# A long convolution on one Trainium2 core: its first step folded over the sign of j and run as four 64 by 64 tiles

## The chip, the cores and the metric

The kernel runs on one core of a Trainium2 chip. The core has five engines that work side by side and wait for each other through semaphores: TensorE (PE in the profile; PEld is its loading of weights), VectorE (DVE), ScalarE (ACT), GpSimd (POOL) and SyncE (SP), which here only issues DMAs. The metric is the device time of one execution in microseconds. A profile is one execution with the hardware profiler on; its span runs from the first to the last instruction.

## The reference

A gated long convolution is followed by a soft mixture of experts over its output. Only the convolution is touched by the change.

```python
h_mlp = np.maximum(pos_emb @ w1, 0.0) @ w2          # S x D filter, S = 11456, D = 128
h_filt = h_mlp * np.exp(-0.01 * np.arange(S))[:, None]
u = x * v                                           # B x S x D, B = 4
y = irfft(rfft(u, n=2*S, axis=1) * rfft(h_filt, n=2*S, axis=0)[None], n=2*S, axis=1)[:, :S]
attn_out = x * y
# then a soft mixture of 8 experts over the B*S rows of attn_out
```

All numbers are fp32.

## The kernel before

**The transform.** A cyclic length of 111 times 197 replaces the FFT. A sequence position is written as 111 j + r + base with j from -52 to 52 (JT = 105 values) and r from 0 to 55 (R = 56), together with its mirror in r. So the input is already folded over the sign of r: `xf` and `vf` hold for each channel a column of 56 values at +r and one at -r. Four steps follow for each group g of 16 channels (CG = 16, with 4 batches C = 64 columns; 8 groups):

- Step 1 (`p1_load`, `p1`): x times v, then sum and difference of the +r and -r columns (`sd`), then a matmul over j against a table of cosines and sines with 99 frequencies k (J = 99). One unit u is 4 columns; a group has 16 units.
- Step 2 (`p2`): for each k one matmul over r with the table W, then the product with the filter's spectrum: two products on VectorE (`m`), a difference and a sum on GpSimd that go back into T. KB = 4 frequencies are one block, so a group has 25 blocks.
- Step 3 (`p3`): the inverse of step 2's sum; 32 calls in a group, two columns each. It takes sums and differences on the way to the big buffer E.
- Step 4 (`p4`): the inverse over k; 14 calls in a group, two for each of 7 blocks rb of 8 values of r. The result is multiplied by x (`xi`) and stored (`p4_out`) to the scratch tensor `scr`.

**The order.** The program runs a loop over g from 0 to 8. In a pass with g from 1 to 7 there are two halves. In the first, unit after unit, step 3 of group g-1 (two calls) stands beside step 1 of group g. In the second, step 4 of group g-1 stands beside step 2 of group g. T is shared: step 1 writes it, step 2 reads it and writes its own result there, step 3 reads that. So step 2 waits for all of step 1, and step 3 of the next pass needs every block of step 2. Before the passes stand the filter's own transform (`hid_step`, `first` with the table `tab1h`, `filter_second`) and group 0, which has only steps 1 and 2 (with `filter_last`, which makes the spectrum). The pass with g = 8 has only steps 3 and 4 of group 7. Behind it runs the mixture of experts.

Within this order a scheduler places the instructions of each engine by its estimate; where the code says `inorder`, program order is kept.

**Buffers.** `ld` holds 5 tiles that x, v and xi share; `st` holds 3 that sd and the outputs xo share. PSUM has two pools of 4 banks: `psa` for steps 1 and 2, `psb` for steps 3 and 4. SyncE issues nearly every DMA from one queue in order, so a load whose buffer isn't free yet holds up what stands behind it.

**How step 1 leaves PSUM.** `first` runs two matmuls with a 105 x 128 weight (56 sums and 56 differences, each padded to 64) against 198 columns (99 cosines, 99 sines). ScalarE then copies in three pieces: lines 130 and 131, and line 135 with the sign turned. For the filter and group 0 the third piece goes to VectorE (line 133).

**How an fp32 matmul looks in the trace.** Each fp32 matmul leaves two records on PE and two on PEld, called passes here: step 3 has 1024 matmuls in the program and 2048 passes.

## Time and profile before

| | us |
|---|---|
| median of 3 runs | 1148.19 (1145.26 to 1152.42) |
| the profiled execution | 1159.05 |
| its span | 1156.9 |
| filter, first step (24.8 to 70.9 of the span) | 46.1 |
| filter, second step (70.9 to 94.7) | 23.8 |
| first half of pass 1 (steps 3 and 1) | 52.4 |
| second half of pass 1 (steps 4 and 2) | 47.4 |
| from the start of pass 1 to the start of pass 8 (7 passes) | 710.0 |
| the mixture of experts (951.9 to the end) | 205.0 |

The borders are the first matmuls of the steps. The profiled execution took 1159.05 us, of which 1156.9 lie between the first and the last instruction; it is 0.9% above the median of the runs. The mixture of experts isn't touched by the change.

The lines that carry the argument stand in the prediction. A group's line gives the line of the kernel, engine, operation, what it writes and reads, shapes, count, then busy time in total and the mean of one, then the engine's idle time before it and who ended it. A line of windows gives for a stretch its length, then each engine's busy time with the number of instructions, the granted TensorE clock, the share of the DMA engines and their rate.

### The profile page before, as it was taken

How to read it: one execution, taken by the hardware profiler on the slowest of the kernel's cores; microseconds unless marked ns; L12 is line 12 of the kernel's file. 1: busy time of each engine (PE TensorE's matmuls, PEld its weight loads, DVE VectorE, ACT ScalarE, POOL GpSimd, SP SyncE). 2: the span in 40 equal slices, each digit the busy share in tenths (PEclk: the TensorE clock that was granted, in tenths of full speed). 3: DMA queues.
4: the chain of work that ended last, by engine and by line, in shares of the span. 5: the costliest groups of instructions: out<-in, count | busy, mean ns of one | idle time of the engine just before them, and what ended most of it. 6: DMA issues, size and time to landing. Idle time of an engine off the chain costs nothing.

```text
span 1156.9 us, 25846 instructions
## 1 busy us (share of the span) xinstructions
PE 1076.8 (93%) x9133; PEld 1005.2 (87%) x9133; DVE 895.9 (77%) x1835; ACT 603.8 (52%) x1496; POOL 603.1 (52%) x742
## 2 busy tenths in 40 slices
PE   6998998999999999999999999999999988997997
PEld 6888898999999899988989998998999986565675
DVE  6336886978779787877977786797778848997797
ACT  1978875920860392087039208703920308776597
POOL 6102486357437544743754474375447004776774
PEclk9689998999999999999999999999999999999998
DMA  8422368624734572474458247345824779774388
GB/s 289 121 80 88 124 228 249 202 79 136 209 112 125 159 229 72 135 210 119 123 154 235 84 133 212 117 125 160 221 80 148 242 208 277 221 220 124 124 353 338
DMA packets 129498, 198.49 MB, mean 172 GB/s; under 512 B 15926, under 2 KB 71537, under 8 KB 129372
## 3 DMA queue, kind: packets, MB, share of 16 engines
q1 hardware_dynamic: 129070, 196.61, 55.7%
q8 instruction: 74, 1.21, 0.5%
q14 instruction: 52, 0.43, 0.1%
q10 hardware_dynamic: 254, 0.11, 0.0%
q0 software_dynamic: 48, 0.13, 0.0%
HBM read 136.90 MB, written 59.90 MB: 170 GB/s over the span
## 4 chain that ended last, share of the span: by engine, by line
PE 40%; issue 21%; DVE 16%; DMA 10%; ACT 9%; POOL 4%; SPq 1%; POOLq 0%; DVEq 0%; ACTq 0%
PE p L284 8%; PE p L236 8%; DMA v<-in_vf_dram 8%; PE p L254 7%; PE p L126 6%; DVE E L260 5%; ACT T L130 4%; PE fl L168 3%; POOL x L218 3%; ACT T L131 3%; PE f L141 2%; PE ct L722 2%; DVE sd L221 2%; DVE xreg L433 2%; DVE xreg L738 1%
## 5 line engine op out<-in xcount | busy, mean ns | idle before, releaser
L258 ACT ACTIVATE ec<-p 99x224 f32<-99x224 f32 x256 | 84.0, 356 | 405.3 <-issue 341.5
L260 DVE TENSOR_TENSOR E<-p,ec 99x224 f32<-99x224 f32 x512 | 221.9, 550 | 43.3 <-ACT ec L258 42.7
L247 POOL TENSOR_TENSOR T<-m,m 111x256 f32<-111x256 f32 (+1 forms) x200 | 146.2, 731 | 187.5 <-DVE m L241 135.8
L241 DVE TENSOR_TENSOR m<-p,T 111x512 f32<-111x512 f32 (+1 forms) x350 | 216.0, 678 | 24.5 <-issue 16.3
L254 PE MATMUL p<-tab,T 111*99 111x112 f32 x2048 | 222.0, 262 | 8.7 <-DVE E L260 4.5
L254 PEld LDWEIGHTS p<-tab,T 111*99 111x99 f32 x2048 | 214.5, 171 | 14.5 <-issue 7.1
L218 POOL TENSOR_TENSOR x<-x,v 112x512 f32<-112x512 f32 x112 | 144.6, 1291 | 157.6 <-DMA v<-in_vf_dram 139.6
L284 PE MATMUL p<-E,tab 99*105 99x128 f32 (+1 forms) x1792 | 215.7, 276 | 11.5 <-DVE E L260 11.5
L126 PE MATMUL p<-tab1x,sd 105*128 105x198 f32 x1024 | 200.8, 342 | 18.7 <-DVE sd L221 16.4
L284 PEld LDWEIGHTS p<-E,tab 99*105 99x105 f32 x1792 | 205.4, 173 | 13.8 <-DVE E L260 11.4
L236 PE MATMUL p<-T,W 128*111 128x128 f32 x1584 | 202.2, 280 | 1.4 <-DVE T L133 1.4
L126 PEld LDWEIGHTS p<-tab1x,sd 105*128 105x128 f32 x1024 | 172.0, 194 | 25.7 <-DVE sd L221 13.0
L236 PEld LDWEIGHTS p<-T,W 128*111 128x111 f32 x1584 | 192.2, 178 | 1.6 <-DVE T L133 1.6
L130 ACT ACTIVATE T<-p 64x396 f32<-64x396 f32 x288 | 163.5, 568 | 33.6 <-PE p L126 29.0
L248 POOL TENSOR_TENSOR T<-m,m 111x256 f32<-111x256 f32 (+1 forms) x200 | 156.7, 783 | 0.0
L221 DVE TENSOR_TENSOR sd<-x 112x256 f32<-112x256 f32 x256 | 113.8, 484 | 55.2 <-POOL x L218 46.1
L290 DVE TENSOR_TENSOR xo<-p,xi 105x256 f32<-105x256 f32 x224 | 84.2, 417 | 47.7 <-PE p L284 34.9
L131 ACT ACTIVATE T<-p 64x198 f32<-64x198 f32 x288 | 106.1, 368 | 3.4
L135 ACT ACTIVATE T<-p 64x198 f32<-64x198 f32 x224 | 74.2, 331 | 0.0
L540 POOL TENSOR_TENSOR E<-lt,mx 128x480 f32<-128x480 f32 (+1 forms) x24 | 24.6, 1026 | 70.0 <-ACT et L522 67.0
L133 DVE TENSOR_SCALAR T<-p 64x198 f32<-64x198 f32 x64 | 27.1, 431 | 43.0 <-ACT T L131 42.5
L726 ACT ACTIVATE cs<-ct 96x512 fp32r<-96x512 f32 x96 | 53.3, 567 | 9.9 <-PE ct L722 6.6
(103 smaller groups left out, 1249.3 us busy)
## 6 DMA issues: line engine op xcount, KB each, us to landing
x<-in_xf_dram SPq DMA_DIRECT2D x128, 224.0 KB
v<-in_vf_dram SPq DMA_DIRECT2D x112, 224.0 KB
xi<-in_xi_dram SPq DMA_DIRECT2D x112, 224.0 KB
out_dram<-xreg SPq DMA_DIRECT2D x22, 960.0 KB
xreg<-scr SPq DMA_DIRECT2D x21, 960.0 KB
scr<-xo SPq DMA_DIRECT2D x104, 192.0 KB
hs<-E SPq DMA_DIRECT2D x12, 1024.0 KB
T<-hs SPq DMA_DIRECT2D x63, 176.0 KB
```

The source lines that it names most:

```text
L126: nc.tensor.matmul(ps[:, i].rearrange("p s k -> p (s k)"), lhsT=src(i), rhs=tab, start=True, stop=True)
L130: nc.scalar.activation(to[0:RP], pq[0:RP], AF.Copy)
L131: nc.scalar.activation(to[RP:128, 0], pq[RP:128, 1], AF.Copy)
L218: inorder(eng.tensor_tensor(out=xt, in0=xt, in1=vt, op=ALU.mult))
L221: add = nc.vector.tensor_tensor(out=sd[:, :, h : h + RP], in0=xt[:, :, 0:RP], in1=xt[:, :, RP:], op=op)
L236: nc.tensor.matmul(ps[:, i].rearrange("p b c -> p (b c)"), lhsT=W[:, k0 + i, :], rhs=Tf[:, :, k0 + i, :], start=True, stop=True)
L241: nc.vector.tensor_mul(m[:, :n].rearrange("p k s c i -> p k (s c i)").rearrange("p k (b c) -> p k b c", c=CG), ps[:, :n], h[:, :, CG * s : ...
L247: nc.gpsimd.tensor_tensor(out=Ty[:, 0], in0=ms[0][:, :n, 0], in1=ms[1][:, :n, 1], op=ALU.subtract)
L248: nc.gpsimd.tensor_tensor(out=Ty[:, 1], in0=ms[1][:, :n, 0], in1=ms[0][:, :n, 1], op=ALU.add)
L254: nc.tensor.matmul(ps[:, i, 2 * s : 2 * s + 2, :].rearrange("p q r -> p (q r)"), lhsT=T[0:N1, s, c // CG, c % CG // 2, :, i], rhs=tab3[:, ...
L260: add = nc.vector.tensor_tensor(out=E[:J, :, 2 * s : 2 * s + 2, c : c + 2].rearrange("p r q c -> p c q r"), in0=ps[:, :, 0:2, :], in1=ec, ...
L284: nc.tensor.matmul(ps[:, i, :n], lhsT=tab4[:, s, o : o + JT], rhs=E[:J, r, s : s + 2 * n - 1 : 2, :], start=(s == 0), stop=(s == 1))
```

## The change

Step 1 is folded over the sign of j too. x times v is followed by two rounds of sum and difference: over the sign of r (from xt into vt) and over the sign of j (from vt back into xt). What is left of j are 53 values (JH), so a unit is a tile of two rows of partitions: columns 0 and 1 in partitions 0 to 52, columns 2 and 3 in partitions 64 to 116. Each column's parts (even or odd in j, even or odd in r) need only the cosines or only the sines: 16 matmuls of 64 x 64 weights against 99 columns in a unit, each at a `tile_position` (64 i, 64 d), instead of 4 of 128 weights against 198. The two rows of tiles write two PSUM banks; the signs lie in the table, which has a third block of negative cosines. ScalarE copies a whole column pair at once.

The filter's `first` splits its 128 weights into two column tiles of 64, whose second reads a shifted table, so that no sign is turned behind it (`filter_first`, four functions f in a call).

Step 3 keeps its even and odd parts: PSUM goes to E with one copy, every third call on VectorE, the others on ScalarE. The sum and difference move behind step 4: ScalarE copies the odd part, VectorE adds and subtracts, and the product with x is one instruction for 8 values of r, on VectorE for the first output and on GpSimd for the second.

Buffers: `ld` has 4, `st` has 4 and takes v, psa has 2 tiles of two banks, and two blocks of step 2 share one.

```diff
-    ld = ctx.enter_context(tc.tile_pool(name="ld", bufs=5))
-    st = ctx.enter_context(tc.tile_pool(name="st", bufs=3))
+    ld = ctx.enter_context(tc.tile_pool(name="ld", bufs=4))
+    st = ctx.enter_context(tc.tile_pool(name="st", bufs=4))
...
-    psa = ctx.enter_context(tc.tile_pool(name="psa", bufs=4, space=bass.MemoryType.PSUM))
+    psa = ctx.enter_context(tc.tile_pool(name="psa", bufs=2, space=bass.MemoryType.PSUM))
...
+    def first(src, tab, ps):
+
+        for h in range(2):
+            nc.tensor.matmul(ps[64 * h : 64 * h + 64], lhsT=src[:, (R - 8) * h : (R - 8) * h + 64],
+                             rhs=tab[:, J * h : J * h + 2 * J], start=True, stop=True,
+                             tile_position=(0, 64 * h))
+
+    def filter_first(f0):
+        ps = psa.tile([128, 2, 512], F32, tag="psa", name=f"f1_{f0}")
+        for h in range(2):
+            for i in range(2):
+                f = f0 + 2 * h + i
+                first(hid[:, :, :, f].rearrange("p s r -> p (s r)"), tab1h,
+                      ps[:, h, 2 * J * i : 2 * J * (i + 1)])
+            f = f0 + 2 * h
+            nc.scalar.activation(Th.rearrange("p k (s f) -> p s k f", s=2)[:, :, :, f : f + 2],
+                                 ps[:, h, : 4 * J].rearrange("p (i s k) -> p s k i", i=2, s=2), AF.Copy)
...
+        shape = [128, 2, 2, 2, R]
+        xt = ld.tile(shape, F32, tag="ld", name=f"x_{g}_{u}")
...
+        vt = st.tile(shape, F32, tag="st", name=f"v_{g}_{u}")
...
-        for h, op in ((0, ALU.add), (RP, ALU.subtract)):
-            add = nc.vector.tensor_tensor(out=sd[:, :, h : h + RP], in0=xt[:, :, 0:RP], in1=xt[:, :, RP:],
-                                          op=op)
...
+        for a, b in ((xt, vt), (vt.rearrange("p c j s r -> p c s j r"), xt.rearrange("p c j s r -> p c s j r"))):
+            for h, op in ((0, ALU.add), (1, ALU.subtract)):
+                add = nc.vector.tensor_tensor(out=b[:, :, :, h], in0=a[:, :, :, 0], in1=a[:, :, :, 1], op=op)
...
     def p1(g, u, sd):
-        for h in range(0, 4, 2):
-            first(lambda i: sd[:JT, h + i, :], tab1x, T[:, :, u // 4, 2 * (u % 4) + h // 2], g == 0)
+        ps = psa.tile([128, 2, 512], F32, tag="psa", name=f"p1_{g}_{u}")
+        for c in range(2):
+
+            for e, d in ((0, 0), (1, 0), (1, 1), (0, 1)):
+                for i in range(2):
+                    w = sd[64 * i : 64 * i + JH, c, e].rearrange("p s r -> p (s r)")
+                    k = 2 * J * c + J * (e ^ d)
+                    nc.tensor.matmul(ps[64 * d : 64 * d + 64, i, k : k + J],
+                                     lhsT=w[:, (R - 8) * d : (R - 8) * d + 64],
+                                     rhs=tab1x[64 * i : 64 * i + JH, J * (e + 2 * (d > e)) : J * (e + 2 * (d > e)) + J],
+                                     start=True, stop=True, tile_position=(64 * i, 64 * d))
+        b, cp0 = u // 4, 2 * (u % 4)
+        for c in range(2):
+            nc.scalar.activation(T[:, :, b, cp0 + c],
+                                 ps[:, :, 2 * J * c : 2 * J * (c + 1)].rearrange("p i (s k) -> p s k i", s=2),
+                                 AF.Copy)
...
-        ec = sm.tile([J, 2, 2, R], F32, tag="ec", name=f"ec_{g}_{c}")
-        nc.scalar.activation(ec, ps[:, :, 2:4, :], AF.Copy)
...
+        to = E[:J, :, :, c : c + 2].rearrange("p r q c -> p q r c")
+        src = ps.rearrange("p c q r -> p q r c")
+        if c // 2 % 3 == 2:
+            nc.vector.tensor_copy(out=to, in_=src)
+        else:
+            nc.scalar.activation(to, src, AF.Copy)
...
+        vt = sm.tile([JT, 4, C], F32, tag="ec", name=f"odd_{g}_{rb}_{h}")
+        nc.scalar.activation(vt, ps[:, :, 1, :], AF.Copy)
+        for s, op in ((0, ALU.add), (1, ALU.subtract)):
+            nc.vector.tensor_tensor(
+                out=xo[s][:, :, 4 * h : 4 * h + 4, :].rearrange("p b r c -> p r b c"),
+                in0=ps[:, :, 0, :].rearrange("p r (b c) -> p r b c", b=B),
+                in1=vt.rearrange("p r (b c) -> p r b c", b=B), op=op)
+        if h:
+            for s, eng in ((0, nc.vector), (1, nc.gpsimd)):
+                eng.tensor_tensor(out=xo[s], in0=xo[s], in1=xs[s][:JT], op=ALU.mult)
```

In the lists below, a name such as `p_0_16_1871` is a tile of PSUM with its group, its column and a running number; `x4` counts matmuls in a row.

TensorE in the first half of pass 1, before: two calls of step 3 (line 254, 8 matmuls), then one unit of step 1 (line 126, 4 matmuls of the full array).

```order
L254 MATMUL p_0_16_1871<-tab_79,T 99x112 x4
L254 MATMUL p_0_18_1880<-tab_79,T 99x112 x4
L126 MATMUL p_72_1889<-tab1x,sd_4_1791 128x198 x2
L126 MATMUL p_73_1895<-tab1x,sd_4_1791 128x198 x2
L254 MATMUL p_0_20_1910<-tab_79,T 99x112 x4
```

The same place now:

```order
L271 MATMUL p_0_16_2000<-tab_82,T 99x112 x4
L271 MATMUL p_0_18_2006<-tab_82,T 99x112 x4
L234 MATMUL p_1_4_2012<-tab1x,x_4_1910 64x99 x16
L271 MATMUL p_0_20_2041<-tab_82,T 99x112 x4
L271 MATMUL p_0_22_2047<-tab_82,T 99x112 x4
```

Each unit's matmuls now stand as 16 small ones in one piece between the full-array matmuls of step 3, so the array changes between full and tiled twice in a unit.

GpSimd at the end of the second half of a pass, before: the last blocks of step 2 (lines 247 and 248, into T), then the products x times v of the next group (line 218).

```order
L247 TENSOR_TENSOR T<-m_2_88_3869,m_2_88_3871 111x4x32x2
L248 TENSOR_TENSOR T<-m_2_88_3871,m_2_88_3869 111x4x32x2
L247 TENSOR_TENSOR T<-m_2_92_3880,m_2_92_3882 111x4x32x2
L248 TENSOR_TENSOR T<-m_2_92_3882,m_2_92_3880 111x4x32x2
L247 TENSOR_TENSOR T<-m_2_96_3890,m_2_96_3892 111x3x32x2
L248 TENSOR_TENSOR T<-m_2_96_3892,m_2_96_3890 111x3x32x2
L218 TENSOR_TENSOR x_0_3930<-x_0_3930,v_0_3932 112x512
L218 TENSOR_TENSOR x_1_3938<-x_1_3938,v_1_3940 112x512
```

The same place now:

```order
L264 TENSOR_TENSOR T<-m_2_88_4106,m_2_88_4108 111x4x32x2
L265 TENSOR_TENSOR T<-m_2_88_4108,m_2_88_4106 111x4x32x2
L309 TENSOR_TENSOR xo_2_6_4138<-xo_2_6_4138,xi_1_6_4084 105x512
L218 TENSOR_TENSOR x_0_4172<-x_0_4172,v_0_4174 128x448
L218 TENSOR_TENSOR x_1_4181<-x_1_4181,v_1_4183 128x448
L264 TENSOR_TENSOR T<-m_2_92_4116,m_2_92_4118 111x4x32x2
L265 TENSOR_TENSOR T<-m_2_92_4118,m_2_92_4116 111x4x32x2
L264 TENSOR_TENSOR T<-m_2_96_4126,m_2_96_4128 111x3x32x2
L265 TENSOR_TENSOR T<-m_2_96_4128,m_2_96_4126 111x3x32x2
```

A product with x (line 309) and the first two products of the next group now stand ahead of the last four writes to T, for which step 3 of the next pass waits.

VectorE at the start of a second half, before: the products with x (line 290) between pairs of step 2's products (line 241).

```order
L290 TENSOR_TENSOR xo_3_0_4551<-p_2_0_1_4590,xi_2_0_4547 105x4x4x16
L290 TENSOR_TENSOR xo_3_0_4552<-p_2_0_1_4590,xi_2_0_4549 105x4x4x16
L241 TENSOR_TENSOR m_3_8_4606<-p_3_8_4601,T 111x512
L241 TENSOR_TENSOR m_3_8_4608<-p_3_8_4601,T 111x512
L241 TENSOR_TENSOR m_3_12_4617<-p_3_12_4612,T 111x512
```

The same place now:

```order
L303 TENSOR_TENSOR xo_3_0_4825<-p_2_0_1_4865,odd_0_1_4874 105x4x4x16
L303 TENSOR_TENSOR xo_3_0_4826<-p_2_0_1_4865,odd_0_1_4874 105x4x4x16
L258 TENSOR_TENSOR m_3_4_4855<-p_3_0_4840,T 111x512
L258 TENSOR_TENSOR m_3_4_4857<-p_3_0_4840,T 111x512
L309 TENSOR_TENSOR xo_3_0_4825<-xo_3_0_4825,xi_2_0_4821 105x512
L258 TENSOR_TENSOR m_3_8_4885<-p_3_8_4880,T 111x512
```

The two instructions on step 4's PSUM stay in number and size and now wait for ScalarE's copy (`odd`); one instruction of 512 elements on SBUF alone (line 309) is added for each block rb.

More of the change, by code (lines that the diff above doesn't have):

```diff
@@ L24 @@
 JP = 112
+JH = JT // 2 + 1
 R = 56
-RP = 64
 FO = 64
+DLO = 128 - R
 G = 8
@@ L120, in hid_step @@
         eng.tensor_tensor(out=hid[:, 1, rs], in0=hb[:, :, 0], in1=hb[:, :, 1], op=ALU.subtract)
-    def first(src, tab, dst, shift):
-        ps = psa.tile([128, 2, 2, J], F32, tag="psa", name=f"p1_{next(ids)}")
-        for i in range(2):
-            nc.tensor.matmul(ps[:, i].rearrange("p s k -> p (s k)"), lhsT=src(i), rhs=tab,
-                             start=True, stop=True)
-        to = dst.rearrange("p s k c -> p s c k")
-        pq = ps.rearrange("p c s k -> p s c k")
-        nc.scalar.activation(to[0:RP], pq[0:RP], AF.Copy)
-        nc.scalar.activation(to[RP:128, 0], pq[RP:128, 1], AF.Copy)
-        if shift:
-            nc.vector.tensor_scalar_mul(to[RP:128, 1], pq[RP:128, 0], -1.0)
-        else:
-            nc.scalar.activation(to[RP:128, 1], pq[RP:128, 0], AF.Copy, scale=-1.0)
+    def first(src, tab, ps):
[13 more added lines that the diff above has]
+                                 ps[:, h, : 4 * J].rearrange("p (i s k) -> p s k i", i=2, s=2), AF.Copy)
     def filter_second(k0):
@@ L191, in conv_part @@
             inorder(nc.sync.dma_start(out=tab1h, in_=t1h))
[L192 to L195 removed]
+    for f in range(0, FO, 4):
+        if f < 44:
+            ks = slice(9 * (f // 4), 9 * (f // 4) + 9)
             inorder(nc.sync.dma_start(out=W[:, ks, :], in_=wt[:, ks, :]))
[L197 removed]
+        filter_first(f)
     for t, q in ((tab1x, t1x), (tab3, t3), (tab4, t4)):
```

81 lines of the change are left out of this document (29 added, 52 removed).

## The prediction

> **What bounds the kernel now.** I read the page's shares first, then a table of windows whose borders are the first matmuls of the steps, then the groups by shape, then short pieces of the timeline.
>
> ```profile
> PE 1076.8 (93%) x9133; PEld 1005.2 (87%) x9133; DVE 895.9 (77%) x1835; ACT 603.8 (52%) x1496; POOL 603.1 (52%) x742
> core 0: us, PE busy (x) PEld busy (x) DVE busy (x) ACT busy (x) POOL busy (x), PEclk, DMA share, GB/s
> 24.80:70.90 46.10, 42.83 (x137) 37.00 (x137) 19.17 (x40) 42.66 (x64) 7.76 (x6) 0.67 0.50 152
> 70.90:94.70 23.80, 23.80 (x198) 23.80 (x199) 3.48 (x8) 14.28 (x28) 0.00 (x0) 0.93 0.07 20
> 94.70:127.00 32.30, 27.03 (x146) 24.46 (x144) 26.44 (x59) 28.52 (x66) 6.74 (x5) 0.95 0.27 80
> 184.60:237.00 52.40, 50.22 (x384) 49.42 (x384) 42.45 (x95) 44.03 (x125) 21.30 (x17) 0.93 0.64 187
> 237.00:284.40 47.40, 47.13 (x422) 47.12 (x422) 41.07 (x78) 1.33 (x5) 34.22 (x50) 1.00 0.39 113
> 488.60:542.00 53.40, 48.38 (x385) 46.60 (x384) 40.68 (x98) 43.40 (x125) 20.88 (x17) 1.00 0.68 186
> 542.00:590.80 48.80, 48.62 (x421) 48.63 (x422) 40.99 (x78) 1.12 (x4) 34.09 (x49) 0.97 0.37 110
> 894.60:922.00 27.40, 25.14 (x257) 24.72 (x256) 26.27 (x67) 11.45 (x32) 0.45 (x1) 1.00 0.80 246
> 922.00:951.90 29.90, 26.27 (x224) 26.10 (x225) 11.37 (x30) 0.52 (x1) 0.00 (x0) 0.94 0.72 208
> ```
>
> The second row is the filter's first step: ScalarE is busy 42.7 of 46.1 us and the TensorE clock falls to 0.67. Then come pairs of halves. The first half (52.4 and 53.4 us, mean 52.9) has three engines over 40 us, none of them full; the second half (47.4 and 48.8, mean 48.1) is TensorE without a gap, VectorE busy 41 us and GpSimd 34 us behind it. Seven such pairs are 710 of 1157 us.
>
> ```profile
> L254 PE MATMUL p<-tab,T 111*99 111x112 f32 x2048 | 222.0, 262 | 8.7 <-DVE E L260 4.5 <-POOL T L247 2.4
> L254 PEld LDWEIGHTS p<-tab,T 111*99 111x99 f32 x2048 | 214.5, 171 | 14.5 <-issue 7.1 <-POOL T L247 2.6 <-POOL T L248 2.3
> L126 PE MATMUL p<-tab1x,sd 105*128 105x198 f32 x1024 | 200.8, 342 | 18.7 <-DVE sd L221 16.4 <-DVE T L133 1.1 <-ACT T L135 0.3
> L130 ACT ACTIVATE T<-p 64x396 f32<-64x396 f32 x288 | 163.5, 568 | 33.6 <-PE p L126 29.0
> L131 ACT ACTIVATE T<-p 64x198 f32<-64x198 f32 x288 | 106.1, 368 | 3.4
> L260 DVE TENSOR_TENSOR E<-p,ec 99x224 f32<-99x224 f32 x512 | 221.9, 550 | 43.3 <-ACT ec L258 42.7
> L218 POOL TENSOR_TENSOR x<-x,v 112x512 f32<-112x512 f32 x112 | 144.6, 1291 | 157.6 <-DMA v<-in_vf_dram 139.6 <-DVE sd L221 9.2 <-DVE E L260 8.9
> L493 ACT ACTIVATE E<-pt 128x512 f32<-128x512 f32 x72 | 40.0, 593 | 10.5 <-PE pt L492 10.4
> L221 DVE TENSOR_TENSOR sd<-x x256: 399/418/1498, 55.7 to 838.0; 112x256 f32<-112x256 f32 x128
> L218 DVE TENSOR_TENSOR x<-x,T x5: 691/692/1332, 61.2 to 119.2; 112x512 f32<-112x512 f32 x5
> L241 DVE TENSOR_TENSOR m<-p,T x350: 546/681/694, 240.2 to 893.1; 111x512 f32<-111x512 f32 x168, 111x384 f32<-111x384 f32 x7
> 895.77 24.08 PE L254 MATMUL p<-tab,T 111*99 111x112 f32 x248
> 505.69 1.58 PE L126 MATMUL p<-tab1x,sd 105*128 105x198 f32 x8 [0.53 <-DVE sd L221]
> 507.11 1.70 PE L254 MATMUL p<-tab,T 111*99 111x112 f32 x16
> 497.92 1.27 POOL L218 TENSOR_TENSOR x<-x,v 112x512 f32<-112x512 f32 x1 [0.57 <-DVE E L260]
> 498.11 1.69 DVE L221 TENSOR_TENSOR sd<-x 112x256 f32<-112x256 f32 x2
> 1014.84 1.40 PE L492 MATMUL pt<-ident,xreg 128*128 128x128 f32 x11
> 1016.17 1.03 PE L500 MATMUL pl<-E,phis 128*32 128x480 f32 x8
> 1017.15 1.07 PE L569 MATMUL pa<-xreg,ev 128*32 128x128 f32 x30
> 1018.15 0.66 PE L492 MATMUL pt<-ident,xreg 128*128 128x128 f32 x4
> ```
>
> Three readings. Passes: step 3's take 24.08/248 = 0.097 us, step 1's eight run from 505.69 to 507.11, 0.178 each. Tiles: 30 passes of the 128 by 32 column tiles, the next block's first matmul 1.00 us behind theirs; the 128-column passes of the full array stand 0.11 apart ((0.66 - 0.33)/3 by the last one's length; eleven before the first tiled block give the same), so one at a time they would take 3.3: four column tiles do run together. The last of those eleven starts about 1.1 us behind the first, the tiled block 1.33 behind it: about 0.2 instead of 0.11, so a change between full and tiled costs 0.1. Port: the sum `sd` that starts at 498.11 while GpSimd multiplies (497.92 to 499.19) ends with its pair at 499.80; alone one takes 418 ns (median), the longest 1498. An instruction of VectorE that reads SBUF alone waits for GpSimd's running one. Products that read PSUM don't (line 241: 681 median, 694 at most, though GpSimd works beside them).
>
> **The change part by part.**
>
> *Filter.* Each two functions cost 568 + 368 ns on ScalarE, then a negation on VectorE; now one copy of 396 elements: line 130 has that size at 568, and between line 131's 368 for 198 and line 493's 593 for 512 lies 510; I take 540. For 32 copies 17 us. TensorE: 64 functions, two passes, 0.178 us, if two column tiles run together as four do above: 22.8 us, in a stretch that then keeps TensorE busy, so I take the full clock. 24 instead of 46.1: -22. The second step had a granted clock of 0.93; -2.
>
> *First half, TensorE, per unit.* Step 3: 16 passes, 16 x 0.097 = 1.55. Step 1: 16 matmuls are 32 passes of 99 columns, half of 198, so 0.089 each. All four tiles always together would be 8 rounds, 0.71; one at a time 32, 2.85. The order of tiles is A B A B C D C D, where a tile returns before all four were used; I count 10 rounds, 0.89. Two changes of mode, 0.2. Sum 2.64.
>
> *First half, the port, per unit.* Four sums of 224 elements, 418 x 224/256 = 366 ns, are 1.46; GpSimd's product is 1291 x 448/512 = 1130 ns. They exclude each other: 2.59 us, before 0.84 + 1.29 = 2.13. TensorE at 2.64 and the port at 2.59 meet.
>
> *First half, the rest.* ScalarE loses line 258 and three pieces per column pair; it gets two copies of 396 (about 0.54) and 4/3 of a copy of 448 to E. The price of those: line 493's 593 for 512 gives 520 without loss; line 260 writes the same scattered E and takes 550 for 224, scaled to 448 that is 1100. With 0.75 taken between, 1.08 + 1.0 = 2.1 per unit: below TensorE, and at the upper end 2.5, still covered. VectorE: 1.46 + 2/3 of such a copy, 2.0. DMA: the same bytes, in 44 instead of 53 us; 186 GB/s becomes some 225, and the windows show 246 elsewhere. x and v now have four units in flight instead of two and a half, so the wait of GpSimd for v (139.6 us) shrinks.
>
> Two resources at 2.6 that wait for each other: I take 2.75 a unit, 44.0 us a half instead of 52.9: -8.9.
>
> *Second half.* TensorE keeps its passes (47 to 49 us). VectorE's instructions on step 4's PSUM keep their number; seven products of 512 on SBUF come, 692 ns each: 41.0 + 4.8 = 45.8. GpSimd runs 34.2/47.4 = 72% of the time, so most of them will first wait for its running instruction, as the sum at 498.11 did. ScalarE's 14 copies (593) have an idle engine, but stand in the chain of each output. GpSimd: 34.2 + 7 x 1.29 = 43.2, + the two products x times v ahead of the last writes to T, 2.3: 45.5, and up to 7 x 0.69 = 4.8 in which VectorE holds the port: 50.3. Its first write to T can't start before about 3.9 us (first product of step 2 at 240.2, 3.2 behind the start of the half, + 0.68). So the next step 3 waits until 49.4 to 54.2; what was covered by TensorE's 48.1 no longer is. I take 52.3, near the middle, since GpSimd is nearly full and each wait passes on to it: +4.2.
>
> *Ends.* Group 0's step 1 is the port alone: before 2 x 0.42 + 1.08 = 1.92 a unit (two products of three on GpSimd), now 4 x 0.366 + 0.95 = 2.41; with four units prepared during the filter, 0 to +6: +3. Pass 8: VectorE's 26.3 of 27.4 goes, TensorE's 24.1 remains: -2. Its last output gets a copy and a product more: +1.5.
>
> **The sum.** 7 x (-8.9 + 4.2) = -32.9; filter -24; ends +2.5: -54.4. Against the profiled 1159.05 that is 1104.7. The runs' median is 10.9 lower; the same difference from 1148.19 gives 1094.
>
> One rule speaks against this. The Trainium skill ("TensorE: Matmul & The Clock Gate", Part 3) says that a weight load overlaps a running matmul only where the row groups differ. Step 3's rows disagree: loads of 171 ns and passes 97 ns apart, both over all rows. By the rule each of the 10 rounds would also carry a load, at most 0.055 us (half of the 0.11 in which a full pass of 128 weights goes through): 1.44, 3.19 a unit, 7 x 7.0 = +49: 1143.
>
> **The rivals.**
> - The second half swallows less: GpSimd's added work falls into its idle 13 us and the half grows by 1. For it: the first half has less to do on GpSimd's side of the seam. 7 x -3.2 = -22: 1072.
> - It swallows more: GpSimd's bound at its upper end, and the three products at the seam (3.5 us) on top where all four last writes queue behind them: +5, 1129.
> - Tiles overlap only in pairs: 16 rounds, 1.42, 3.17 a unit, 50.7 a half: 7 x 6.7 = +47, 1141. For it: A and B alternate and share their columns; no row shows two row tiles at once.
> - Slower: weight loads of the tiles take turns. 32 loads of up to 0.055 are 1.76 a unit, 3.51 with the rest, 56.2 a half: 7 x 12.2 = +85, 1179. Against it only the column tiles, four loads of 32 in 0.11, which fits one after the other too. It decides where step 1 takes 0.49 us a unit more than I count (54.4/112).
> - The change doesn't do what it says: no tiles together. 2.85, 4.6 a unit, 73.6 a half, +207, and the filter keeps its 46: 1321.
>
> **How the numbers follow.** Forecast 44 in 100, less swallowed 15, more 12, pairs 12, the page's rule 3, loads in turn 10, no overlap 4. About 1% is what a measurement here tells from no change; that puts the border at 1137. Faster: 44 + 15, 9 of the 12 at 1129, 4 of the pairs, 1 of the rule: 73. Same: the 12 that are left of these. Slower: 14 and one: 15. The range, 1050 to 1150, leaves out the last two rivals and a little beyond 1072; it takes in the page's.
>
> **What would show it.** A pass of 99 columns near 0.09 with about 1.1 us between the last pass of one step 3 and the first of the next; a first half near 44 with TensorE and VectorE both waiting; sums of VectorE with long ones among them; a second half of 52 in which GpSimd is busy over 90% and step 3 starts on line 265; the filter's first step at 24 with a clock near 1. If the tiled passes spread over 1.5 us or more in a unit, the gain is gone; if the second half stays at 48, it is larger.

## The result, and the profile after

The changed kernel takes 1246.7 us (median of 4 runs, 1242.9 to 1256.2), the kernel before in the same comparison 1147.4: 1.087 times the time, with a 95% interval of 1.080 to 1.094. The prediction was 1094, faster, with a range from 1050 to 1150: the kernel became slower where it was to become faster.

The page of the changed kernel, shares of the span (1246.2 us):

```profile
PE 1077.6 (86%) x12333; PEld 967.5 (78%) x12333; DVE 847.3 (68%) x1651; ACT 480.4 (39%) x1016; POOL 683.9 (55%) x797
```

TensorE is busy for as long as before (1076.8) in a span 89 us longer, although step 1 gives it less work; ScalarE and VectorE have less to do. So the time went into waiting, and part of TensorE's busy time into passes at a lower clock: the mean granted clock is 0.925 over the span, where it was 0.962. Where, a table of windows says; its columns are those of the prediction's table and its borders again the first matmuls of the steps: the filter's first step, group 0, the two halves of pass 4.

```profile
22.30:59.10 36.80, 30.91 (x276) 25.08 (x276) 7.85 (x17) 14.79 (x32) 3.79 (x3) 0.95 0.57 194
...
81.40:181.70 100.30, 84.75 (x989) 78.61 (x988) 72.56 (x125) 54.76 (x106) 51.87 (x58) 0.86 0.58 187
521.10:578.50 57.40, 47.96 (x769) 42.80 (x769) 31.06 (x71) 25.85 (x52) 17.32 (x15) 0.90 0.50 150
578.50:635.80 57.30, 49.48 (x424) 48.03 (x422) 49.10 (x89) 6.26 (x16) 48.39 (x59) 0.93 0.39 116
```

Passes 1 to 7 run from 181.7 to 979.9 us, 798.2 against 710.0 before. Over the whole span, stage by stage in us (the last two columns are kernels of the experiments, "three edits" and "best"):

| stage | before | predicted | after | three edits | best |
|---|---|---|---|---|---|
| ahead of the filter | 24.8 | 24.8 | 22.3 | 23.3 | 22.5 |
| filter, first step | 46.1 | 24.1 | 36.8 | 27.6 | 28.4 |
| filter, second step | 23.8 | 21.8 | 22.3 | 22.4 | 22.4 |
| group 0 | 89.9 | 92.9 | 100.3 | 92.9 | 92.8 |
| passes 1 to 7 | 710.0 | 677.1 | 798.2 | 698.4 | 674.9 |
| of that a first half, mean | 53.1 | 44.0 | 57.0 | 50.2 | 46.9 |
| and a second half, mean | 48.3 | 52.3 | 57.0 | 49.5 | 49.5 |
| pass 8 and the mixture | 262.3 | 261.8 | 266.3 | 264.4 | 260.7 |
| span | 1156.9 | 1102.5 | 1246.2 | 1129.0 | 1101.7 |

(Means are over the seven passes; the two pairs that the prediction shows have means of 52.9 and 48.1. "Predicted" is its terms set against the span.)

A row of the groups and some of the list of waits name the places. In the list stand the total, the number of waits and the longest:

```profile
L218 POOL TENSOR_TENSOR x<-x,v 128x448 f32<-128x448 f32 x123 | 145.0, 1185 | 287.2 <-DMA x<-in_xf_dram 187.0
```

```profile
DVE v L221 <- POOL x L218: 170.5, 67, 22.9
PE p L271 <- DVE E L277: 48.4, 28, 4.3
PE p L271 <- POOL T L264: 47.7, 8, 6.8
PE p L253 <- DVE m L258: 14.2, 22, 1.5
```

Over the whole span GpSimd waits 187.0 us for loads of x and 41.3 for v, where it was 28.6 and 139.6. In passes 1 to 7 alone it is 114.7 and 40.5, 155.2 together, against 139.6 before, all of it for v: the wait for v shrinks, the one for x takes its place, and the sum grows. The sums on VectorE wait for GpSimd, and step 3's matmuls (line 271) for copies to E that stand on VectorE behind those sums. In eight places, once for each group, step 3 waits up to 6.8 us for the last writes to T.

**The first half.** The timeline of SyncE's queue and of GpSimd in pass 4 (start, duration, and in brackets the idle time before):

```profile
545.07 0.33 SPq L216 DMA_DIRECT2D v<-in_vf_dram  x1
...
547.85 0.35 SPq L212 DMA_DIRECT2D x<-in_xf_dram  x1
554.39 0.33 SPq L216 DMA_DIRECT2D v<-in_vf_dram  x1
```

```profile
550.92 1.13 POOL L218 TENSOR_TENSOR x<-x,v 128x448 f32<-128x448 f32 x1 [6.46 <-PE p L271]
552.50 1.27 POOL L218 TENSOR_TENSOR x<-x,v 128x448 f32<-128x448 f32 x1 [0.45 <-DMA x<-in_xf_dram]
```

Loads go out in bursts of two units, 9.3 us apart (545.07, 554.39). Before, at a place like it, they went out one unit at a time, 2.1 to 3.0 us apart:

```profile
506.84 0.31 SPq L216 DMA_DIRECT2D v<-in_vf_dram  x1
...
509.79 0.31 SPq L216 DMA_DIRECT2D v<-in_vf_dram  x1
```

The order of the program says which load is which. SyncE in the first half of a pass, after the change (the first number behind x or v is the unit; the loads of the filter's spectrum between them are left out):

```
L216 DMA v_9_5656<-in_vf_dram 128x448
...
L212 DMA x_7_5572<-in_xf_dram 128x448
L216 DMA v_10_5697<-in_vf_dram 128x448
...
L212 DMA x_8_5613<-in_xf_dram 128x448
```

From unit 6 on, x of unit u stands behind v of unit u+2, and that v waits for its buffer (`st` has four), which the sums of unit u-2 free. The buffers are there for four units, but the queue lets only two be under way: sums of one pair, load, product, sums of the next pair, about 9 us for two units.

**The end of the second half.** TensorE and GpSimd from 509 to 521 us:

```profile
509.43 1.07 PE L253 MATMUL p<-T,W 128*111 128x128 f32 x8
512.03 0.91 PE L253 MATMUL p<-T,W 128*111 128x128 f32 x6 [1.53 <-DVE m L258]
513.14 1.17 PE L253 MATMUL p<-T,W 128*111 128x128 f32 x8 [0.20 <-DVE m L258]
521.10 2.14 PE L271 MATMUL p<-tab,T 111*99 111x112 f32 x8 [6.79 <-POOL T L264]
```

```profile
515.24 1.27 POOL L309 TENSOR_TENSOR xo<-xo,xi 105x512 f32<-105x512 f32 x1
516.46 2.22 POOL L218 TENSOR_TENSOR x<-x,v 128x448 f32<-128x448 f32 x2
518.63 0.88 POOL L264 TENSOR_TENSOR T<-m,m 111x256 f32<-111x256 f32 x1
```

All of step 4 is done when the last three blocks of step 2 run (22 passes), so nothing is left to cover the last writes to T; and three products of GpSimd stand ahead of four of these. Before, 32 passes of step 4 stood behind the last block of step 2:

```profile
587.44 3.66 PE L284 MATMUL p<-E,tab 99*105 99x128 f32 x32
```

Note too what the last two blocks of step 2 wait for: VectorE's products (line 258).

**The filter.** TensorE in the first step:

```profile
34.51 1.79 PE L128 MATMUL f<-tab1h,E 99*64 99x198 f32 x16 [0.46 <-ACT T L140]
36.75 1.79 PE L128 MATMUL f<-tab1h,E 99*64 99x198 f32 x16 [0.45 <-ACT T L140]
```

Matmuls and copies (line 140) take turns: four functions every 2.25 us.

**The clock in the passes.** In the wait of 6.79 us at the seam the granted clock falls to 0.50, and it stays there for the first 4.6 us of the next first half:

```profile
519.00:525.00 6.00, 3.90 (x24) 3.40 (x28) 3.98 (x7) 0.79 (x2) 2.93 (x5) 0.50 0.44 128
```

More drops follow behind the waits within a first half. Its mean granted clock over the seven passes is 0.87, where it was 0.99 before; with the loads in turn it is 0.92, with three edits 0.91, in the best kernel 0.93.

### The profile page after: what moved, and what is told of

The parts are those of the page before. It is cut to its first block, busy times and chain, and to the rows that moved or that the text cites. A ratio compares the mean times of both kernels' runs of the same rounds, so it can differ in the third digit from the quotient of the medians.

```text
span 1246.2 us, 31259 instructions
## 1 busy us (share of the span) xinstructions
PE 1077.6 (86%) x12333; PEld 967.5 (78%) x12333; DVE 847.3 (68%) x1651; ACT 480.4 (39%) x1016; POOL 683.9 (55%) x797
## 3 DMA queue, kind: packets, MB, share of 16 engines
q1 hardware_dynamic: 133190, 196.72, 50.4%
## 5 line engine op out<-in xcount | busy, mean ns | idle before, releaser
L271 PE MATMUL p<-tab,T 111*99 111x112 f32 x2048 | 268.5, 292 | 96.3 <-DVE E L277 48.4
L218 POOL TENSOR_TENSOR x<-x,v 128x448 f32<-128x448 f32 x123 | 145.0, 1185 | 287.2 <-DMA x<-in_xf_dram 187.0
L221 DVE TENSOR_TENSOR v<-x 128x224 f32<-128x224 f32 x256 | 117.8, 501 | 170.6 <-POOL x L218 170.5
L253 PE MATMUL p<-T,W 128*111 128x128 f32 x1584 | 217.9, 279 | 14.3 <-DVE m L258 14.2
L297 PE MATMUL p<-E,tab 99*105 99x128 f32 x1792 | 221.7, 273 | 0.6 <-ACT E L279 0.6
L279 ACT ACTIVATE E<-p 99x448 f32<-99x448 f32 x176 | 99.7, 567 | 229.1 <-PE p L271 227.0
L234 PE MATMUL p<-tab1x,x 53*64 53x99 f32 x4096 | 144.7, 280 | 13.8 <-DVE x L221 12.9
L240 ACT ACTIVATE T<-p 128x396 f32<-128x396 f32 x256 | 114.0, 499 | 100.8 <-PE p L234 100.6
L234 PEld LDWEIGHTS p<-tab1x,x 53*64 53x64 f32 x4096 | 118.2, 151 | 32.4 <-issue 10.2
L303 DVE TENSOR_TENSOR xo<-p,odd 105x256 f32<-105x256 f32 x224 | 83.6, 413 | 55.2 <-ACT odd L301 53.0
L221 DVE TENSOR_TENSOR x<-v 128x224 f32<-128x224 f32 x256 | 108.8, 466 | 6.7 <-PE p L234 0.5
L309 POOL TENSOR_TENSOR xo<-xo,xi 105x512 f32<-105x512 f32 x56 | 74.1, 1322 | 47.1 <-issue 33.4
```

The lines of the kernel that those rows point to most:

```text
L218: inorder(eng.tensor_tensor(out=xt, in0=xt, in1=vt, op=ALU.mult))
L221: add = nc.vector.tensor_tensor(out=b[:, :, :, h], in0=a[:, :, :, 0], in1=a[:, :, :, 1], op=op)
L234: nc.tensor.matmul(ps[64 * d : 64 * d + 64, i, k : k + J], lhsT=w[:, (R - 8) * d : (R - 8) * d + 64], rhs=tab1x[64 * i : 64 * i + JH, J * ...
L240: nc.scalar.activation(T[:, :, b, cp0 + c], ps[:, :, 2 * J * c : 2 * J * (c + 1)].rearrange("p i (s k) -> p s k i", s=2), AF.Copy)
L253: nc.tensor.matmul(ps[:, i].rearrange("p b c -> p (b c)"), lhsT=W[:, k0 + i, :], rhs=Tf[:, :, k0 + i, :], start=True, stop=True)
L271: nc.tensor.matmul(ps[:, i, 2 * s : 2 * s + 2, :].rearrange("p q r -> p (q r)"), lhsT=T[0:N1, s, c // CG, c % CG // 2, :, i], rhs=tab3[:, ...
```

## The experiments

Each edit is to the changed kernel, and each run stands against the kernel before on the same chip, where that one took 1142.5 to 1150.8 us; the runs are on several chips, so differences of under 1% between them say little. The halves are means over passes 1 to 7, from the first matmul of step 3 to the first of step 4, and on to the next step 3; the filter's first step ends where its second begins.

| run | us | ratio to before (95%) | first half | second half | filter |
|---|---|---|---|---|---|
| the change | 1246.7 | 1.087 (1.080 to 1.094) | 57.0 | 57.0 | 36.8 |
| loads in turn | 1170.1 | 1.022 (1.015 to 1.029) | 46.1 | 57.1 | 38.0 |
| second half as written | 1406.4 | 1.228 (1.221 to 1.235) | 57.7 | 79.1 | 37.8 |
| filter as written | 1264.6 | 1.106 (1.098 to 1.114) | 56.1 | 57.0 | 58.0 |
| these three | 1379.8 | 1.205 (1.196 to 1.213) | 50.4 | 79.8 | 58.0 |
| filter, tile per pair | 1232.9 | 1.074 (1.064 to 1.084) | 55.4 | 57.0 | 29.0 |
| GpSimd's end | 1242.9 | 1.085 (1.080 to 1.089) | 59.3 | 54.2 | 37.5 |
| GpSimd's and TensorE's end | 1228.4 | 1.073 (1.068 to 1.078) | 56.9 | 55.2 | 38.1 |
| step 2, tile per block | 1180.8 | 1.030 (1.023 to 1.038) | 55.5 | 49.5 | 36.9 |
| three edits | 1132.2 | 0.987 (0.983 to 0.991) | 50.2 | 49.5 | 27.6 |
| + copies on ScalarE | 1110.9 | 0.968 (0.964 to 0.972) | 48.4 | 49.5 | 28.5 |
| + tiles in the cyclic order | 1125.3 | 0.980 (0.976 to 0.984) | 50.5 | 49.5 | 29.0 |
| + both (best) | 1104.8 | 0.962 (0.959 to 0.966) | 46.9 | 49.5 | 28.4 |

**Loads in turn.**

```diff
         dma = nc.sync.dma_start(out=xt, in_=xf[g, u])
-        if g == 0:
+        if g == 0 or u >= 2:
             inorder(dma)
...
-        nc.sync.dma_start(out=vt, in_=vf[g, u])
+        inorder(nc.sync.dma_start(out=vt, in_=vf[g, u]))
```

> The changed kernel, but each load of v stands behind its own load of x in SyncE's queue, and each x (from unit 2 on) behind the v ahead of it. Nothing else is changed. Theory A (order of the load queue): in the changed kernel x of unit u stands behind v of unit u+2, which waits until the sums of unit u-2 have freed its buffer, so only two units are in flight and a unit takes up to 4.8 us; with the loads in turn, four are, the first half falls from a mean of 57.0 to about 46 us, the second stays at 57.3, and 7 x 11 = 77 us go: 1170. Theory B (the copies to E on VectorE stand behind sums and hold up step 3; TensorE waits 48 us for them in the profile): the loads alone bring less than 25 us, over 1220. Theory C (the port between VectorE and GpSimd is full): the first half stays over 54 us and the time within 1% of 1247.

Measured 1170.1; the first half falls to 46.1, the second stays at 57.1. Group 0 falls a little too, to 97.7, and the filter's first step is 38.0. Pass 4's first half, from the table of windows, and its loads:

```profile
492.50:536.80 44.30, 44.30 (x769) 40.13 (x769) 29.22 (x71) 25.93 (x52) 17.78 (x15) 0.95 0.65 194
```

```profile
508.12 0.33 SPq L212 DMA_DIRECT2D x<-in_xf_dram  x1
508.49 0.43 SPq L216 DMA_DIRECT2D v<-in_vf_dram  x1
...
510.73 0.33 SPq L212 DMA_DIRECT2D x<-in_xf_dram  x1
```

A unit's loads go out every 2.6 us, and TensorE works without a gap, 44.3 of 44.3 us. Theory A holds in mechanism and size. B and C fall: with the same copies on VectorE and the same port, TensorE's wait for line 277 falls from 48.4 us to 1.6. It was a consequence of the loads. What the half has over 16 units of 2.62 us (41.9) is the lower clock at its start: 0.95 of 44.3 us are 42.1.

**The order of the second half, as written.**

```diff
-            nc.tensor.matmul(ps[:, i].rearrange("p b c -> p (b c)"), lhsT=W[:, k0 + i, :],
-                             rhs=Tf[:, :, k0 + i, :], start=True, stop=True)
+            mm = nc.tensor.matmul(ps[:, i].rearrange("p b c -> p (b c)"), lhsT=W[:, k0 + i, :],
+                                  rhs=Tf[:, :, k0 + i, :], start=True, stop=True)
+            if g:
+                inorder(mm)
...
-                nc.tensor.matmul(ps[:, i], lhsT=tab4[:, s, o : o + JT], rhs=E[:J, r, s::2, :],
-                                 start=(s == 0), stop=(s == 1))
+                inorder(nc.tensor.matmul(ps[:, i], lhsT=tab4[:, s, o : o + JT], rhs=E[:J, r, s::2, :],
+                                         start=(s == 0), stop=(s == 1)))
```

GpSimd's two writes to T (lines 264 and 265) and its product of the second output (line 309) are put in `inorder` in the same way.

> The changed kernel, but the matmuls of steps 4 and 2 on TensorE, and on GpSimd the writes to T and the products of the outputs, stand in the order in which the program has them; so 32 passes of step 4 come behind the last of step 2, as before the change, and GpSimd's last writes to T stand ahead of the last product and the next group's. Theory D (order at the seam): in the changed kernel the last 22 passes are step 2's, three products of GpSimd stand ahead of the last four writes, and TensorE has nothing to do for 7.1 us; with the order put back 6 of these go in each of seven passes, the second half comes to 51 us: 1247 - 42 = 1205. Rival E (GpSimd is simply full: busy 48.4 of 57.3 us): the order changes where TensorE waits, not how long, and the second half stays at 56 or more: over 1237.

Measured 1406.4, far over both: the second half is 79.1 us. TensorE in that second half:

```profile
670.75 1.16 PE L253 MATMUL p<-T,W 128*111 128x128 f32 x8
673.46 1.17 PE L253 MATMUL p<-T,W 128*111 128x128 f32 x8 [1.55 <-DVE m L260]
```

A block of step 2 (8 passes) waits until VectorE's products have read the block ahead of it. Both blocks lie in one PSUM tile, in different banks; the second does not touch what the products read, but its wait is for the tile. Where the two stand directly behind each other, as here, TensorE stops. The scheduler had kept them apart with step 4's passes, and had paid with the end of the half.

**The filter's matmuls as written.**

```diff
-            nc.tensor.matmul(ps[64 * h : 64 * h + 64], lhsT=src[:, (R - 8) * h : (R - 8) * h + 64],
+            inorder(nc.tensor.matmul(ps[64 * h : 64 * h + 64], lhsT=src[:, (R - 8) * h : (R - 8) * h + 64],
```

> The changed kernel, but the matmuls of the filter's first step stand on TensorE in the order in which the program has them. In the changed kernel three matmuls of block n+1 stand ahead of the last four of block n, and wait for a buffer that block n-1's copies free: matmuls (1.46 us) and copies (0.7 us with the way there) take turns, 2.25 us a block of four functions. Theory F: in order they overlap, a block takes the larger of 1.46 and about 1.0, the step falls from 35.9 to about 24 us, and the time by 12: 1235. Rival G (two blocks of buffers are too few whatever the order, or the stream of W and of the hidden layer sets the pace): the step stays over 33 us and the time at 1247.

Measured 1264.6, the step 58.0 us: theory F is wrong. It is the same fault as in the run before: one tile holds two pairs of functions, and the second pair's matmuls wait for the copy of the first. The rest of the loss goes with a lower clock, told at the end.

**These three edits together.**

> The three edits together: loads in turn, the order of TensorE and GpSimd in the second half as written, the filter's matmuls in order. If theories A, D and F hold, and add, 77 + 42 + 12 = 131 us go: 1116, faster than the kernel before (1147). If the port or GpSimd is the limit (C, E), it stays over 1200. If the halves hand their waits on to each other, it comes to between.

Measured 1379.8: the three do not add. The edits to the order carry their losses along; the first half keeps most of what the loads gave.

**A PSUM tile for each pair of the filter's functions.**

```diff
-        ps = psa.tile([128, 2, 512], F32, tag="psa", name=f"f1_{f0}")
         for h in range(2):
+            ps = psa.tile([128, 512], F32, tag="psa", name=f"f1_{f0}_{h}")
```

> The changed kernel, but in the filter's first step each pair of functions has a PSUM tile of its own; in the changed kernel two pairs share one, and the second pair's matmuls wait until the first pair's copy has read the tile. Theory F2 (the shared tile, not the order, makes matmuls and copies take turns: the order alone made it worse): now the copy of one pair runs beside the matmuls of the next, two pairs take about 1.45 us instead of 2.25, the step falls from 36 to about 25 us, the time by 11: 1236. Rival G2 (the loads of W, the copies, or a clock that stays at half as in the run before set the pace): the step stays over 33 us, and the time within 0.5% of 1247.

Measured 1232.9 (three of the four runs 1222.4 to 1238.0, one 1242.3), the step 29.0 us. F2 holds: passes follow each other without a gap, here 34 in 3.54 us.

```profile
33.77 3.54 PE L128 MATMUL f<-tab1h,E 99*64 99x198 f32 x34
```

```profile
22.00:30.00 8.00, 7.92 (x54) 6.21 (x56) 0.00 (x0) 3.05 (x6) 0.00 (x0) 0.60 1.02 409
30.00:40.00 10.00, 10.00 (x102) 8.73 (x98) 1.56 (x2) 6.20 (x12) 2.37 (x2) 0.98 0.91 278
```

At 102 passes in 10 us the step's 256 passes are 25.1 us. Most of what is over that is the first 8 us, at a granted clock of 0.60.

**The end of the second half, GpSimd alone, then TensorE too.** In the first run only the marked product is held in order; in the second step 4's matmuls with rb = 6 as well.

```diff
-                eng.tensor_tensor(out=xo[s], in0=xo[s], in1=xs[s][:JT], op=ALU.mult)
+                mul = eng.tensor_tensor(out=xo[s], in0=xo[s], in1=xs[s][:JT], op=ALU.mult)
+                if s and rb == 6 and g < G - 1:
+                    inorder(mul)
```

> The changed kernel, but in each of the first seven passes GpSimd's last product of an output stands behind its last four writes to T, and with it the next group's first two products of x and v. Theory D (three products ahead of the writes hold up step 3): the writes end some 3.5 us earlier, the second half falls from 57.4 to about 54, 7 x 3.5 = 24 us go: 1222. Rival H (what the seam gains, the next group's first units lose, since their products come 3.5 us later): the first half grows by as much as the second loses, 1240 to 1250.

> The edit of the run before, and on TensorE the 32 passes of the last block of step 4 stand behind the last pass of step 2 in the first seven passes, as they stood before the change. Theory D in full: those passes (3.5 us) run while GpSimd does its last writes to T, and of the 7.1 us in which TensorE has nothing to do at most 1 is left: second half about 51, 7 x 6.4 = 45 us go: 1202. Rival E (GpSimd is full over the whole half, busy 48.4 of 57.3 us): it ends no earlier than in the run before, and the time equals that run's.

Measured 1242.9 and 1228.4. GpSimd alone: the second half loses 2.8 us, the first grows by 2.3, as rival H has it; the whole is within 0.5% of the change. With TensorE's order too, the second half is 55.2, not 51: theory D is wrong in size. The last pass of step 2 still starts only 50.3 to 52.7 us into the half, as in the changed kernel (50.3), because it waits for its tile (TensorE waits 31.0 us for line 258 in this run, 14.2 in the changed kernel); passes put behind it only come later.

**A PSUM tile for each block of step 2.**

```diff
-        if k0 % (2 * KB) == 0:
-            p2ps[0] = psa.tile([N1, 2, KB, 2 * B, CG], F32, tag="psa", name=f"p2_{g}_{k0}")
-        ps = p2ps[0][:, k0 // KB % 2]
+        ps = psa.tile([N1, KB, 2 * B, CG], F32, tag="psa", name=f"p2_{g}_{k0}")
```

> The changed kernel, but each block of step 2 has a PSUM tile of its own, two in flight, instead of two blocks in each of two tiles; no order is written down. Theory K (the pairing is the cause of the order at the seam: the second block of a tile has to wait until the products of the first have read it, and so the scheduler puts the last three blocks behind all of step 4): without the pairs the last matmuls are step 4's again, the second half falls to 49 to 52 us, 7 x 6 = 42 us go: 1205. Rival L (two tiles in flight are too few, and pairing was the better choice): the second half grows to over 60, the time to over 1260.

Measured 1180.8, with fewer blocks in flight (two instead of four) and no order written down. Every second half is 49.5 us, its last pass of step 2 starts 46.7 us in, and group 0 takes 94.0 instead of 100.3. The end of pass 3's second half on TensorE (its lines 251, 295 and 269 are the change's 253, 297 and 271):

```profile
486.79 0.85 PE L251 MATMUL p<-T,W 128*111 128x128 f32 x6
487.48 1.04 PE L295 MATMUL p<-E,tab 99*105 99x128 f32 x8
490.18 4.15 PE L269 MATMUL p<-tab,T 111*99 111x112 f32 x25 [1.66 <-POOL T L262]
```

Now the scheduler itself leaves passes of step 4 behind step 2, and GpSimd's writes to T stand ahead of the next group's products. Theory K holds, and the order at the seam is explained by the pairing: nothing else was changed. The edit gave more than the 42 us of theory K, since the first halves (57.0 to 55.5) and group 0 gained too.

**The three edits that worked, together; then two more.** Loads in turn, a tile per pair in the filter, a tile per block of step 2. Then with every copy to E on ScalarE, or with the loop over (e, d) in the order (0, 0), (0, 1), (1, 0), (1, 1), so that tiles follow as A B C D A B C D, then with both.

> Three edits to the changed kernel together, each measured alone before: loads of x and v in turn (1170 alone), a PSUM tile for each block of step 2 (1181), a PSUM tile for each pair of functions in the filter (1233). If they work on three different stretches they add: against 1247 they gave 77, 66 and 14 us, so 1090, first half 46, second 49.5, filter's first step 28; faster than the kernel before the change by 5%. If the halves hand their waits on to each other (a faster second half leaves less time to load ahead, a faster first half finds GpSimd still busy), the first half comes to 50 or more and the time to over 1115.

> The kernel of the run before, with all copies to E on ScalarE (one in three was on VectorE). Theory B' (what is left over 44 us in the first half is step 3's wait for copies that stand behind sums on VectorE): the first half falls from 46 to 43 to 44 us, 15 to 20 us less than the run before. Rival M (the port between VectorE's sums and GpSimd's products, or ScalarE, sets the pace): no change or slower, since VectorE's copies read PSUM and ScalarE gets 0.57 us x 11 more a half.

> The kernel with the three edits, with step 1's tiles issued in the order A C B D instead of A B A B C D C D. The prediction counted 10 rounds of 0.089 us for the order of the change and 8 for a cyclic one; the profile of the changed kernel shows 32 passes in about 0.73 us, as 8 rounds would be. If the order of tiles matters (10 rounds), a unit gains 0.18 us, 7 x 16 x 0.18 = 20 us where TensorE is the bound. If not (each tile has its own queue of weights and passes), the time equals that of the kernel with the three edits within 0.5%.

> The three edits, all copies to E on ScalarE, and step 1's tiles in the cyclic order. The profiles with one of the last two gave units 2.615 us apart (order of the change) and 2.562 (cyclic) where TensorE sets the pace, and first halves of 48.4 us with the copies on ScalarE. If both hold, 7 x 16 x 0.053 = 6 us go at most from 1111: 1105 to 1111, steady units of 2.56 us. Rival: where the port sets the pace (2.59 us by the prediction), units stay at 2.6 and the time is that of the kernel with the copies moved, 1111, or more.

Measured 1132.2, 1110.9, 1125.3 and 1104.8. The three do not add: the first half is 50.2, not 46, and the time is over 1115, as for halves that hand their waits on to each other. At the start of pass 4 with three edits, TensorE and then GpSimd:

```profile
463.56 6.64 PE L269 MATMUL p<-tab,T 111*99 111x112 f32 x48 [1.66 <-POOL T L262]
...
476.94 0.39 PE L234 MATMUL p<-tab1x,x 53*64 53x99 f32 x4 [0.92 <-DVE x L221]
```

```profile
475.25 3.77 POOL L218 TENSOR_TENSOR x<-x,v 128x448 f32<-128x448 f32 x3 [4.66 <-DMA v<-in_vf_dram]
```

In the changed kernel the first two products of a group were done in the 7 us in which TensorE stood still (516.46 above); now they fall into the first half (466.14 and 469.22), and the third waits 4.66 us for its load of v. The waits are not all: behind them the clock falls to 0.50 for 10 us, in which 16 passes of step 3 take 3.02 us instead of 1.78 and a unit 4.53 (486.84 to 491.37):

```profile
481.00:491.00 10.00, 9.45 (x128) 8.34 (x121) 7.11 (x18) 4.14 (x9) 4.21 (x4) 0.50 0.86 266
```

```profile
486.84 1.65 PE L234 MATMUL p<-tab1x,x 53*64 53x99 f32 x32
488.43 3.02 PE L269 MATMUL p<-tab,T 111*99 111x112 f32 x16
491.37 0.97 PE L234 MATMUL p<-tab1x,x 53*64 53x99 f32 x32
```

At full clock, later in the half, units stand 2.6 us apart: 499.22 and 501.84 here, 489.64 and 492.20 in the best kernel.

```profile
499.22 0.97 PE L234 MATMUL p<-tab1x,x 53*64 53x99 f32 x32
500.12 1.78 PE L269 MATMUL p<-tab,T 111*99 111x112 f32 x16
501.84 0.97 PE L234 MATMUL p<-tab1x,x 53*64 53x99 f32 x32
```

```profile
489.64 0.92 PE L234 MATMUL p<-tab1x,x 53*64 53x99 f32 x32
490.49 1.78 PE L269 MATMUL p<-tab,T 111*99 111x112 f32 x16
492.20 0.92 PE L234 MATMUL p<-tab1x,x 53*64 53x99 f32 x32
```

The copies on ScalarE give 21 us (14 between the two profiled executions), about what B' said, but its mechanism is not shown: with three edits TensorE waits only 1.4 us in all for copies on VectorE, and the first half falls to 48.4, not to 43 or 44. What falls is TensorE's wait for the sums of step 1, from 31.6 to 24.0 us. The cyclic order shortens a steady unit from 2.62 to 2.56 us, a third of the 0.18 that was forecast if the order matters. The first halves are no shorter for it (50.5 against 50.2); the whole time is 0.6% below that of the three edits, with intervals that touch, so only the trace tells it. The best kernel ends 3.8% below the kernel before. What is left of the late start (the third load of v waits for a buffer in `st` that an output still holds, by the order of the program) was not tried.

## Why the prediction was wrong, step by step

- **The loads of the first half: the step that failed most.** "x and v now have four units in flight instead of two and a half, so the wait of GpSimd for v (139.6 us) shrinks": the buffers were counted, the order of SyncE's queue was not read. Two units were in flight. The wait for v did shrink, to 40.5 us in the passes, but one of 114.7 for x stood in its place, and a half took 57.0 us instead of 44.0. With the loads in turn it was 46.1.
- **The clock of the passes: a term put at nothing.** The sum priced TensorE at its full clock, as the halves before had it (0.99). Each new wait also lowered the clock, to a mean of 0.87 in a first half. What that cost by itself no run separates; in the best kernel it is 0.93, and if TensorE set the pace all the while, 0.07 of 46.9 us would be some 3 us a half (an estimate).
- **The second half: a term that the sum lacked.** The +4.2 was made of GpSimd's added work, "Its first write to T can't start before about 3.9 us", and products at the seam. That two blocks of step 2 share a tile stood in the diff and got no price. It cost 7.5 us a half (57.0 to 49.5). The added work that was priced is nearly hidden: 49.5 without the pairing, so the rival "swallows less", at 49.1, was right about it. The rival "swallows more" had named the three products at the seam; the run with GpSimd's end alone shows that they were not the cause: the half falls by 2.8 us and the whole by 0.3%, and the last block of step 2 comes late with or without them.
- **The filter: the same omission.** "One copy of 396 elements" took about 0.50, not 0.54, and tiles ran together; but the two pairs of one tile take turns with their copies. 36.8 instead of 24.1; 27.6 to 29.0 with tiles of their own. The rest is passes at 0.098 us (102 in 10 us) where 0.089 was taken, and the clock at the start.
- **TensorE's work per unit: right, in part by luck.** 2.64 predicted, 2.62 measured where TensorE sets the pace. Two terms are off and cancel: the tiles with one change of mode take 0.90, not 0.99, and step 3 with the other takes 1.72 (500.12 to 501.84), not 1.65. Ten rounds were too many: the 32 passes start within about 0.73 us. The tiles run together: 32 passes and the change of mode take 0.90 us up to the next step 3, where the rivals had 1.42 (pairs), 1.76 (loads in turn) and 2.85 (none together), all without the change of mode. By the rule of the Trainium skill ("TensorE: Matmul & The Clock Gate", Part 3), that a load overlaps a matmul only where their row groups differ, the unit would have been 3.19; the trace does not agree.
- **The port: right in place, not the bound.** In pass 4 of the changed kernel two sums take 0.69 us alone (at 546.17) and 1.43 while GpSimd multiplies (at 552.88), so a sum does wait for GpSimd's product; but with the loads in turn a unit goes at TensorE's pace, 2.62, and in the best kernel at 2.56, below the 2.59 that was counted for the port.
- **Copies to E: cheaper than priced.** 0.75 was taken for 448 elements, with 1.1 from line 260 as the upper end; the group of line 279 shows 0.567 on ScalarE.
- **Group 0**: +3 predicted, +10.4 measured, and +3.0 with the three edits. Most of the difference is the pairing (94.0 with that edit alone).
- **The sum.** With the three edits the passes take 698 us instead of the 677 predicted: a first half 6.2 us more than the 44.0, a second 2.8 less than the 52.3. What is missing is the start of each first half, its waits and the clock behind them. Apart from the three products at the seam no rival named a wait for order, and none a shared tile or the clock; they priced engines. That was the fault of the prediction as a whole: it took work for time, and the program's order, which was at hand, was read for TensorE and GpSimd at two places only. (The rival with no tiles together adds up to 1323, not 1321: 1094, 207 and the filter's 22. Nothing rests on it.)

## What to carry to other kernels

When a change moves buffers, read the order of every queue that feeds them, the DMA queue first: what is in flight is what the queue lets pass, not what the pool has room for. Two independent results in one PSUM tile cost a wait for each other's readers, and the scheduler here moved step 4 and the end of a half around that wait; give each its own tile before touching the order. A stall of one engine may hide another's preparation, so gains of neighbouring stages should not be added. Read the granted clock of each stage beside its busy time: busy time does not tell work from work at half the clock.

## What the runs showed of the hardware

**The clock.** In the run with the filter's matmuls as written, the granted clock stayed at 0.50 for the whole of the first step:

```profile
30.00:40.00 10.00, 8.20 (x48) 4.99 (x46) 0.00 (x0) 3.02 (x6) 0.33 (x1) 0.50 1.00 319
```

```profile
43.26 2.95 PE L128 MATMUL f<-tab1h,E 99*64 99x198 f32 x16 [0.62 <-ACT T L140]
```

There TensorE works for 2.95 us and then waits 0.6, busy over 80% of the time. In the changed kernel the same matmuls begin with 7.5 us without a gap (22.25 to 29.75), the clock is 1.00 from 30 us on, and it stays there through waits of 0.46 us after every 1.8. A reading that fits both, and that no run tests: at half clock the matmuls are so long that their own waits break every stretch before the clock is up. The Trainium skill ("TensorE: Matmul & The Clock Gate", Part 1) says that the full clock comes after about 3.4 us of sustained work and goes after an idle window of that length. On the way up both runs agree with it (2.95 us are not enough, 7.5 are). On the way down the passes do not: with three edits a wait of 1.66 us (ahead of 463.56) is enough for the half clock.

```profile
464.00:467.00 3.00, 3.00 (x16) 2.89 (x16) 0.60 (x1) 0.55 (x1) 2.55 (x3) 0.50 0.84 258
```

**The order of tiles.** Four 64 by 64 tiles at work together: 32 passes take 0.90 us up to the next step in the order A B A B C D C D and 0.85 in the cyclic one.
